# The last weight rows of a decode layer accumulated by column halves in two PSUM banks, with the output copy split over two engines

## The chip, the cores and the metric

One Trainium2 chip, one core. The time is the device time of the core in microseconds (us). "Span" is the part of the run that the profile covers (136.1 us of 138.0 for the kernel before). PE is TensorE (PEld its weight loads), DVE VectorE, ACT ScalarE, SP SyncE; L485 is line 485 of the kernel, and lines move by a few between versions.

## The reference, cut to what matters

One decode step of a transformer layer for four sequences: attention over the last 2048 cached positions, then a gated MLP. Only the end matters here:

```python
h  = x + attention(layernorm(x))          # h is h1 in the kernel, [4, 1024]
h_ = silu(hn @ w1) * (hn @ w3)            # hn = layernorm(h); w1, w3: 1024 x 3584
h2 = h + h_ @ w2                          # w2: 3584 x 1024, all bfloat16
```

## The kernel before

The kernel keeps a ring in SBUF and streams all weights and the cache through it in one fixed order on SyncE's DMA queue. w2 comes last, as 28 "rows" (one row is 128 partitions x 1024 columns), in four loads:

```python
("w2", load_rows, (56 * KIB, w2_v, D, 0, 17)),     # rows 0 to 16
("w2", load_rows, (90 * KIB, w2_v, D, 17, 7)),     # rows 17 to 23
("w2", load_rows, (104 * KIB, w2_v, D, 24, 3)),    # rows 24 to 26
("w2", load_rows, (110 * KIB, w2_v, D, 27, 1)),    # row 27
```

The 1024 output columns are folded into four groups of 256, one to each strip of 32 partitions, so that one row is four matmuls with 32 columns of weights each, which run side by side: within a row of the first load the four start within 34 ns of each other and the record of each lasts 0.37 to 0.42 us, while rows follow each other every 213 ns at a granted clock of 0.50. h1 enters the accumulation early, through a matmul with an fp32 identity. At the end ScalarE copies the PSUM bank and issues the store:

```python
# early, while VectorE computes the layernorm statistics
nc.tensor.matmul(y2_ps[:], lhsT=ident_f[:], rhs=h1[:], start=True, stop=False, ...)
# ... gate and up projections, hgT = transposed product ... (cut)
for i in range(IF):                       # 28 rows of w2
    for j in range(JG):                   # 4 strips
        nc.tensor.matmul(y2_ps[QD * j : QD * (j + 1), :], lhsT=hgT[:, i, :],
                         rhs=loaded["w2"][i][:, j * CG : (j + 1) * CG],
                         start=False, stop=(i == IF - 1), ...)
res = act.tile([P, CG], BF16)
nc.scalar.copy(out=res[:], in_=y2_ps[:])
nc.scalar.dma_start(out=out_flat..., in_=res[0:P:RS, :])
```

## Time and profile before

| Kernel before | value |
|---|---|
| time, median of 3 runs | 138.03 us (137.88 to 138.03) |
| read from HBM | 55.59 MB, 408 GB/s over the span |
| PE, DVE, ACT busy | 54%, 32%, 23% of the span |
| last load's landing to the issue of the store | 0.77 us |

Two rows of the page of the kernel before: the span in 40 slices, each digit a busy share (or granted clock) in tenths.

```profile
PEclk9999999999999999997555555579757777555577
DMA  5999999999999999999979999989899999989970
```

The DMA engines are nearly full from the second slice to almost the last (9 in most slices, 7 at the lowest); no compute engine is busy in all of them (PE, the busiest, 54%). The chain of work that ended last, of the kernel before, from 95 us on (start us, us, what):

```profile
75.97 22.91 DMA ring<-in_B_w_dram
98.88 0.04 issue
98.92 2.41 PE g_ps L455 x17
...
101.46 31.31 DMA ring<-in_B_w_dram
132.77 0.04 issue
132.81 0.32 PE y_ps L485 x4
133.13 0.02 issue
133.15 0.37 ACT res L495
```

So the kernel is a stream of bytes, and only what comes after the last byte can be shortened by work on the engines: four matmuls (0.32 us), one copy (0.37 us) and the store. The timeline of the kernel before at its end (start, duration, engine, line, operation, count, and in brackets the idle time before it and what ended it):

```profile
126.09 3.82 PE L485 MATMUL y_ps<-ring,hgT 128*32 128x256 bf16 x68 [7.08 <-DMA ring<-in_B_w_dram]
...
130.34 1.22 PE L485 MATMUL y_ps<-ring,hgT 128*32 128x256 bf16 x28 [0.43 <-DMA ring<-in_B_w_dram]
...
132.18 0.92 PE L485 MATMUL y_ps<-ring,hgT 128*32 128x256 bf16 x16 [0.63 <-DMA ring<-in_B_w_dram]
...
133.15 0.37 ACT L495 CAST res<-y_ps 128x256 bf16<-128x256 f32 x1 [26.41 <-PE y_ps L485]
133.55 0.60 ACTq L496 DMA_DIRECT2D out_dram<-res  x1
```

PE waits for the data of rows 0, 17 and 24. The third line holds rows 24 to 26 and row 27 together; the chain above shows that row 27 began at 132.81. PE thus has room of its own before row 24 (0.63 us).

### The profile page before, as it was taken

How to read it: one execution, taken by the hardware profiler on the slowest of the kernel's cores; microseconds unless marked ns; L12 is line 12 of the kernel's file. 1: busy time of each engine (PE TensorE's matmuls, PEld its weight loads, DVE VectorE, ACT ScalarE, POOL GpSimd, SP SyncE). 2: the span in 40 equal slices, each digit the busy share in tenths (PEclk: the TensorE clock that was granted, in tenths of full speed). 3: DMA queues.
4: the chain of work that ended last, by engine and by line, in shares of the span. 5: the costliest groups of instructions: out<-in, count | busy, mean ns of one | idle time of the engine just before them, and what ended most of it. 6: DMA issues, size and time to landing. Idle time of an engine off the chain costs nothing.

```text
span 136.1 us, 2343 instructions
## 1 busy us (share of the span) xinstructions
PE 73.8 (54%) x1050; PEld 45.0 (33%) x1050; DVE 43.4 (32%) x79; ACT 31.1 (23%) x36; POOL 1.7 (1%) x8
## 2 busy tenths in 40 slices
PE   0202980979898989810535906793096440900960
PEld 0200220267474747400024905571043210300840
DVE  6820000044243434471984001206100695080000
ACT  3000000016555555518385200000002300000001
POOL 5000000000000000000000000000000000000000
PEclk9999999999999999997555555579757777555577
DMA  5999999999999999999979999989899999989970
GB/s 156 463 464 404 404 438 405 424 428 438 433 428 419 429 443 428 429 522 477 462 327 443 481 409 404 477 371 477 354 430 426 438 455 442 430 389 419 421 288 5
DMA packets 2789, 55.75 MB, mean 410 GB/s; under 512 B 311, under 2 KB 471, under 8 KB 731
## 3 DMA queue, kind: packets, MB, share of 16 engines
q1 hardware_dynamic: 2731, 55.58, 95.6%
q8 instruction: 8, 0.13, 0.3%
q10 hardware_dynamic: 48, 0.02, 0.1%
q14 instruction: 2, 0.02, 0.0%
HBM read 55.59 MB, written 0.01 MB: 408 GB/s over the span
## 4 chain that ended last, share of the span: by engine, by line
DMA 54%; PE 24%; ACT 11%; DVE 5%; SPq 2%; issue 1%; ACTq 0%
DMA ring<-in_B_w_dram 40%; DMA ring<-in_A_wq_dram 15%; PE kt_ps L315 10%; ACT kT L321 5%; PE scores_ps L300 5%; ACT z L356 3%; PE q_ps L259 3%; SPq L119 2%; PE g_ps L455 2%; DVE rmax L332 2%; ACT Pm L337 2%; PE OT_ps L378 2%; DVE pT L346 1%; DVE z L352 1%; ACT L337 1%
## 5 line engine op out<-in xcount | busy, mean ns | idle before, releaser
L321 ACT COPY kT<-kt_ps 128x1024 bf16<-128x1024 bf16 x16 | 15.9, 1013 | 13.1 <-PE kt_ps L315 13.1
L315 PE MATMUL kt_ps<-ident,ring 128*128 128x128 bf16 x256 | 17.8, 230 | 0.0
L315 PEld LDWEIGHTS <-ring 128*128 128x128 bf16 x256 | 15.8, 104 | 4.9 <-issue 4.9
L319 DVE COPY kT<-kt_ps 128x1024 bf16<-128x1024 bf16 x16 | 11.1, 692 | 16.2 <-PE kt_ps L315 16.2
L259 PE MATMUL q_ps<-ring,xnT 128*4 128x512 bf16 x63 | 7.2, 626 | 10.5 <-DMA ring<-in_A_wq_dram 10.5
L378 PE MATMUL OT_ps<-z,ring 128*128 128x32 bf16 x256 | 7.5, 188 | 9.0 <-ACT z L356 5.0
L455 PEld LDWEIGHTS <-hnT 128*32 128x32 bf16 x128 | 5.3, 137 | 19.3 <-issue 16.6
L300 PE MATMUL scores_ps<-kT,qz 128*32 128x512 bf16 x64 | 9.9, 610 | 2.9 <-ACT kT L321 2.9
L455 PE MATMUL u_ps<-ring,hnT 128*32 128x448 bf16 x64 | 6.4, 576 | 8.2 <-DMA ring<-in_B_w_dram 8.2
L378 PEld LDWEIGHTS <-ring 128*128 128x128 bf16 x256 | 7.4, 105 | 9.8 <-issue 9.7
L485 PE MATMUL y_ps<-ring,hgT 128*32 128x256 bf16 x112 | 5.8, 375 | 8.3 <-DMA ring<-in_B_w_dram 8.1
L455 PE MATMUL g_ps<-ring,hnT 128*32 128x448 bf16 x64 | 5.5, 529 | 5.2 <-DMA ring<-in_B_w_dram 5.2
L485 PEld LDWEIGHTS <-hgT 128*32 128x32 bf16 x112 | 4.5, 130 | 10.2 <-issue 5.9
L259 PEld LDWEIGHTS <-xnT 128*4 128x4 bf16 x63 | 2.0, 115 | 14.8 <-issue 14.7
L277 DVE TENSOR_SCALAR q_sb<-q_ps 128x512 bf16<-128x512 f32 x1 | 0.7, 692 | 19.5 <-PE q_ps L259 19.5
L495 ACT CAST res<-y_ps 128x256 bf16<-128x256 f32 x1 | 0.4, 372 | 26.4 <-PE y_ps L485 26.4
L356 ACT ACTIVATE z<-pt_ps,mask 128x512 bf16<-128x512 f32 x8 | 5.3, 687 | 3.5 <-DVE z L352 3.5
L348 PE MATMUL pt_ps<-pT,perm 128*128 128x512 bf16 x4 | 2.4, 608 | 6.8 <-DVE pT L346 6.8
L278 ACT ACTIVATE q_sb<-q_ps 128x512 bf16<-128x512 f32 x1 | 0.6, 597 | 23.6 <-DVE q_sb L277 23.6
L405 PE MATMUL y_ps<-ring,o 128*32 128x256 bf16 x128 | 5.5, 352 | 0.8 <-DVE o L394 0.8
L352 DVE TENSOR_SCALAR z<-pt_ps,mask 128x512 bf16<-128x512 f32 x8 | 5.5, 738 | 1.2 <-ACT z L356 0.8
L469 DVE RECIPROCAL eg<-eg 128x896 f32<-128x896 f32 x1 | 5.8, 5754 | 0.0
(79 smaller groups left out, 50.2 us busy)
## 6 DMA issues: line engine op xcount, KB each, us to landing
ring<-in_A_k_cache_dram SPq DMA_DIRECT2D x4, 2048.0 KB, 25.4
ring<-in_A_v_cache_dram SPq DMA_DIRECT2D x4, 2048.0 KB, 39.0
ring<-in_B_w_dram SPq DMA_DIRECT2D x1, 7168.0 KB
ring<-in_B_w_dram SPq DMA_DIRECT2D x2, 3584.0 KB, 23.3
ring<-in_B_w_dram SPq DMA_DIRECT2D x1, 4352.0 KB
ring<-in_A_wq_dram SPq DMA_DIRECT2D x1, 4096.0 KB, 12.1
ring<-in_A_wq_dram SPq DMA_DIRECT2D x1, 3968.0 KB, 19.8
ring<-in_B_w_dram SPq DMA_DIRECT2D x1, 1792.0 KB
```

The source lines that it names most:

```text
L259: nc.tensor.matmul(q_ps[QD * g : QD * g + B, hf * 512 : hf * 512 + n], lhsT=xnT[:, kc, :], rhs=wq_t[:, c0 : c0 + n], start=(kc == 0), stop ...
L300: nc.tensor.matmul(scores_ps[QD * g : QD * (g + 1), n * 512 : (n + 1) * 512], lhsT=qz_v[:, z0 : z0 + QD], rhs=kT_v[:, g, :, :], start=(b = ...
L315: nc.tensor.transpose(out=kt_ps[:, jj, :], in_=k_v[:, n * NJ + t * TB + jj, :], identity=ident[:])
L319: nc.vector.tensor_copy(out=kT[:, t * TB : (t + 1) * TB, :], in_=kt_ps[:])
L321: nc.scalar.copy(out=kT[:, t * TB : (t + 1) * TB, :], in_=kt_ps[:])
L352: nc.vector.tensor_scalar(out=z[:, :, g, :], in0=pt_ps[:], scalar1=mask[:, g : g + 1], scalar2=None, op0=ALU.mult)
L356: nc.scalar.mul(out=z[:, :, g, :], in_=pt_ps[:], mul=mask[:, g : g + 1])
L378: nc.tensor.matmul(OT_ps[:, b, :], lhsT=loaded["v"][b][:, j, :], rhs=PTz[j // NJ][:, (j % NJ) * B + b, :, :], start=(j == 0), stop=(j == J ...
L405: nc.tensor.matmul(y_ps[QD * j : QD * (j + 1), :], lhsT=o4[:, i, :, :].rearrange("p b s -> p (b s)"), rhs=loaded["wo"][i][:, j * CG : (j + ...
L455: nc.tensor.matmul(out_ps[QD * j : QD * (j + 1), hf, :HF], lhsT=hnT[:, k, :], rhs=loaded[kind][k][:, c0 : c0 + HF], start=(k == 0), stop=( ...
L469: nc.vector.reciprocal(out=eg[:], in_=eg[:])
L485: nc.tensor.matmul(y2_ps[QD * j : QD * (j + 1), :], lhsT=hgT[:, i, :], rhs=loaded["w2"][i][:, j * CG : (j + 1) * CG], start=False, stop=(i ...
```

## The change

The intent: shorten the copy after the last matmul by giving half the columns to VectorE and half to ScalarE. The two halves lie in two PSUM banks, one for each engine; that the second bank is needed was the assumption. To keep the bulk of the rows in whole-width matmuls, rows 0 to 16 go into the freed bank `y`, VectorE adds h1 to them, and the sum joins the two halves through the fp32 identity after row 23.

```diff
-    y2_ps = psB.tile([P, CG], FP32, tag="y2")
+    HC = CG // 2
+    ya_ps = psB.tile([P, 512], FP32, tag="ya")
+    yb_ps = psB.tile([P, 512], FP32, tag="yb")
...
-    nc.tensor.matmul(y2_ps[:], lhsT=ident_f[:], rhs=h1[:], start=True, ...)
...
+    y2_ps = psB.tile([P, CG], FP32, tag="y")
+    h2 = wide.tile([P, CG], FP32, tag="w4k")
+    # down(i, n, c0, out_ps): the four strips of row i, n columns from c0 (cut)
+    for i in range(R1):                                   # R1, R2 = 17, 24
+        down(i, CG, 0, y2_ps, start=(i == 0), stop=(i == R1 - 1))
+    nc.vector.tensor_tensor(out=h2[:], in0=y2_ps[:], in1=h1[:], op=ALU.add)
+    for i in range(R1, IF):
+        for c, t in enumerate((ya_ps, yb_ps)):
+            down(i, HC, c * HC, t, start=(i == R1), stop=(i == IF - 1), ...)
+        if i == R2 - 1:
+            for c, t in enumerate((ya_ps, yb_ps)):
+                nc.tensor.matmul(t[:, :HC], lhsT=ident_f[:],
+                                 rhs=h2[:, c * HC : (c + 1) * HC], start=False, stop=False, ...)
-    nc.scalar.copy(out=res[:], in_=y2_ps[:])
+    nc.vector.tensor_copy(out=res[:, :HC], in_=ya_ps[:, :HC])
+    nc.scalar.copy(out=res[:, HC:], in_=yb_ps[:, :HC])
```

More of the change, by code (lines that the diff above doesn't have):

```diff
@@ L80 @@
     RING = 5 * 16384
+    R1, R2 = 17, 24
     RQ = 4
@@ L445 @@
     )
-    nc.tensor.matmul(y2_ps[:], lhsT=ident_f[:], rhs=h1[:], start=True, stop=False, skip_group_check=True)
     def gate_up(kind, out_ps):
@@ L480, with down @@
     )
-    for i in range(IF):
+    y2_ps = psB.tile([P, CG], FP32, tag="y")
+    h2 = wide.tile([P, CG], FP32, tag="w4k")
+    def down(i, n, c0, out_ps, **kw):
         for j in range(JG):
             nc.tensor.matmul(
-                y2_ps[QD * j : QD * (j + 1), :],
+                out_ps[QD * j : QD * (j + 1), :n],
                 lhsT=hgT[:, i, :],
-                rhs=loaded["w2"][i][:, j * CG : (j + 1) * CG],
-                start=False,
-                stop=(i == IF - 1),
-                skip_group_check=True,
-            )
+                rhs=loaded["w2"][i][:, j * CG + c0 : j * CG + c0 + n],
+                **kw,
+            )
+    for i in range(R1):
[3 more added lines that the diff above has]
+        for c, t in enumerate((ya_ps, yb_ps)):
+            down(i, HC, c * HC, t, start=(i == R1), stop=(i == IF - 1), skip_group_check=True)
+        if i == R2 - 1:
+            for c, t in enumerate((ya_ps, yb_ps)):
+                nc.tensor.matmul(
+                    t[:, :HC], lhsT=ident_f[:], rhs=h2[:, c * HC : (c + 1) * HC],
+                    start=False, stop=False, skip_group_check=True,
+                )
     res = act.tile([P, CG], BF16)
-    nc.scalar.copy(out=res[:], in_=y2_ps[:])
+    nc.vector.tensor_copy(out=res[:, :HC], in_=ya_ps[:, :HC])
+    nc.scalar.copy(out=res[:, HC:], in_=yb_ps[:, :HC])
     nc.scalar.dma_start(out=out_flat.rearrange("b (j c) -> j b c", j=JG), in_=res[0:P:RS, :])
```

## The prediction

> **What bounds the kernel now.** Bytes. The page gives 55.59 MB read at 408 GB/s over a 136.1 us span; its DMA row is at 9 in most slices. From 76 us on the chain of waits is two DMA pieces (22.9 and 31.3 us) with 2.4 us of gate matmuls between, while the queue still has a backlog. The weights of w2 come last. In the timeline PE waits for each piece: rows 0 to 16 start at 126.09, 17 to 23 at 130.34, 24 to 26 at 132.18, row 27 at 132.81. The exposed tail starts there: four 256-column matmuls (0.32 us), a ScalarE copy of 128x256 (0.37 us), issue of the store at 133.55, and 2.5 us of store and end, untouched.
>
> **What the change does.** The loads, their order and waits stay the same, so row 27 should land at about 132.8 again. Off the path it removes the fp32 identity matmul at 92.3 us (0.70 us on PE; nobody waits for it) and adds a 128x256 VectorE add after row 16 (the residual add of that shape took 425 ns), done long before it is needed.
>
> *Saved on the path.* The final copy becomes two 128x128 copies on two engines. A ScalarE copy of 128x128 from PSUM took 265 ns here, against 372 ns for 128x256; VectorE handled 128x128 from PSUM in 292 ns and may start about 50 ns earlier. Saving about 0.1 us. The last row is eight matmuls of half the columns: same streaming.
>
> *Added, perhaps on the path.* Rows 17 to 27 double their instructions (44 more weight loads and matmuls). The four column strips run together: rows follow each other every 107 to 110 ns at clock 1.00 and 213 ns at 0.50[...]. I expect half rows at 55 to 65 ns, as 128-wide weight loads with 32 columns go by every 27 ns in attention. But a weight load's record lasts 92 to 97 ns (150 at half clock); if that can't overlap two half rows deep, a row costs about 200 ns. Then two fp32 identity matmuls of 128 columns come between rows 23 and 24. One of 256 columns took 0.70 us, so two of 128 are estimated at 0.6 to 0.8 us[...].
>
> Before, PE ended rows 17 to 23 at 131.56 and idled 0.63 us. The identity pair about fills that gap: row 24 starts near 132.3 rather than 132.18, rows 24 to 26 issue in 0.35 us, still before row 27 lands. So nothing is added. In the bad case PE is late by 0.5 to 0.7 us at the end.
>
> **Prediction.** 138.0 us (about 0.1 saved, against a chance of one in four of losing 0.3 to 0.7), 137.6 to 138.7 in 8 of 10. Faster by over 2%: 0.01; within 2%: 0.98; slower: 0.01.
>
> **What would show it.** Right: PE idle before row 27 with DMA as releaser; the chain ends DMA, eight matmuls, ScalarE copy of about 0.27 us, store issued about 0.1 us earlier after the landing; half rows 55 to 65 ns apart at full clock. Wrong: no DMA wait before row 27, PE back to back from row 17 to the end.
>
> **What would make it wrong.** A low granted clock in the last 6 us (it rose from 0.50 to 1.00 only at 130.94; later, and the identity pair and half rows cost twice as much);[...] weight loads that bind; or DMA time differing by more than the 0.1 us seen between runs.

The pair's 0.6 to 0.8 us held extra cost, with no figure of its own; the figure that is shown is the 0.70 us of one identity matmul of 256 columns. The pair was set against the 0.63 us gap before row 24 and counted as nothing added, so the sum came to the 138.03 us of the kernel before, less about 0.1, with a chance of one in four of losing 0.3 to 0.7: put down as 138.0. The 50 ns by which VectorE may start earlier were an estimate without a stated source; 0.06 us were measured.

## More of the kernel before

In the waits of the kernel before, PE has a long one for which no releaser is named ("issue"; the columns are us in total, times, and the longest):

```profile
PE OT_ps L378 <- issue: 4.0, 1, 4.0
```

## The result, and the profile after

The changed kernel took 137.87 us (median of 6 runs, 137.77 to 137.94), the kernel before 138.03 us in the same rounds (6 runs, 137.86 to 138.07). The ratio is 0.9991, with a 95% interval of 0.9978 to 1.0003. Ratios here are the mean time of one kernel's fast runs over that of the other's of the same rounds, so not quite the ratio of the medians quoted beside them.

The chain of work that ended last, of the changed kernel, from 95 us on:

```profile
98.95 2.41 PE g_ps L456 x17
...
101.49 31.30 DMA ring<-in_B_w_dram
132.79 0.04 issue
132.83 0.24 PE ya_ps L489 x4
133.07 0.08 PE yb_ps L489 x4
133.16 0.02 issue
133.18 0.27 ACT res L511
```

Up to the last landing nothing moved: 132.79 us here, 132.77 before. The matmuls of row 27 take 0.32 us in sum, as before, and the copy 0.27 us in place of 0.37. The timeline of the changed kernel at its end:

```profile
130.37 0.30 PE L489 MATMUL ya_ps<-ring,hgT 128*32 128x128 bf16 x4 [0.34 <-DMA ring<-in_B_w_dram]
...
130.68 0.23 PE L489 MATMUL ya_ps<-ring,hgT 128*32 128x128 bf16 x4
130.74 0.23 PE L489 MATMUL yb_ps<-ring,hgT 128*32 128x128 bf16 x4
130.79 0.23 PE L489 MATMUL ya_ps<-ring,hgT 128*32 128x128 bf16 x4
...
131.35 0.49 PE L504 MATMUL ya_ps<-h,ident_f 128*128 128x128 f32 x2
...
131.67 0.39 PE L504 MATMUL yb_ps<-h,ident_f 128*128 128x128 f32 x2
...
132.21 0.24 PE L489 MATMUL ya_ps<-ring,hgT 128*32 128x128 bf16 x4 [0.15 <-DMA ring<-in_B_w_dram]
...
132.83 0.24 PE L489 MATMUL ya_ps<-ring,hgT 128*32 128x128 bf16 x4
...
132.89 0.24 PE L489 MATMUL yb_ps<-ring,hgT 128*32 128x128 bf16 x4
133.12 0.29 DVE L510 CAST res<-ya_ps 128x128 bf16<-128x128 f32 x1 [2.62 <-PE yb_ps L489]
133.18 0.27 ACT L511 CAST res<-yb_ps 128x128 bf16<-128x128 f32 x1 [26.60 <-PE yb_ps L489]
133.49 0.60 ACTq L512 DMA_DIRECT2D out_dram<-res  x1
```

A half row is the four matmuls of 128 columns of one row that go to one bank. Half rows follow each other 55 to 56 ns apart once the clock is up. The identity pair sits in what was idle time before row 24, and PE still waits 0.15 us for that row's data. VectorE starts its half 0.06 us ahead of ScalarE and both end within 0.04 us.

From the issue of the store to the end of the span takes 2.57 us in both traces (133.554 to 136.125 us before, 133.486 to 136.060 after), so the store issued 0.07 us earlier ended the span 0.07 us earlier.

The whole saving is small against the scatter of a run, so I use a measure from the trace that the scatter of the DMA hardly touches (0.678, 0.678 and 0.679 us in the three traces of the changed kernel), the **tail**: from the instant at which SyncE's record in the trace shows the last load as landed (0.02 to 0.03 us ahead of row 27's first matmul where PE is waiting) to the start of the store's issue. It is 0.767 us before and 0.678 us after: 0.089 us less.

### The profile page after: what moved, and what is told of

Same layout as the page of the kernel before. It is cut to its first block, busy times and chain, and to the rows that moved or that the text cites. A ratio compares the mean times of both kernels' runs of the same rounds, so it can differ in the third digit from the quotient of the medians.

```text
span 136.1 us, 2438 instructions
## 1 busy us (share of the span) xinstructions
PE 72.9 (54%) x1096; PEld 45.1 (33%) x1096; DVE 44.1 (32%) x81; ACT 31.0 (23%) x36; POOL 1.7 (1%) x8
## 4 chain that ended last, share of the span: by engine, by line
DMA 55%; PE 23%; ACT 11%; DVE 5%; SPq 2%; issue 1%; ACTq 0%
DMA ring<-in_B_w_dram 40%; DMA ring<-in_A_wq_dram 15%; PE kt_ps L316 10%; ACT kT L322 5%; PE scores_ps L301 5%; ACT z L357 3%; PE q_ps L260 3%; SPq L120 2%; PE g_ps L456 2%; DVE rmax L333 2%; ACT Pm L338 2%; PE OT_ps L379 2%; DVE pT L347 1%; DVE z L353 1%; ACT L338 1%
## 5 line engine op out<-in xcount | busy, mean ns | idle before, releaser
L489 PE MATMUL y_ps<-ring,hgT 128*32 128x256 bf16 x68 | 3.8, 418 | 7.2 <-DMA ring<-in_B_w_dram 7.2
```

Of the source, the lines that this page charges most:

```text
L489: nc.tensor.matmul(out_ps[QD * j : QD * (j + 1), :n], lhsT=hgT[:, i, :], rhs=loaded["w2"][i][:, j * CG + c0 : j * CG + c0 + n], **kw,)
```

## The experiments

All outputs were correct. Each tail is that of one traced execution. Times are medians of 5 or 6 runs, ratios are to the kernel before on the same chip and rounds.

| Run | what it is | tail, us | median, us | ratio (95%) |
|---|---|---|---|---|
| kernel before | | 0.767 | 138.03 | |
| changed kernel, e0_after | again | 0.678 | 137.95 | 0.9995 (0.9981 to 1.0009) |
| changed kernel, e11_after_again | and again | 0.679 | 137.79 | 0.9986 (0.9974 to 0.9999) |
| e1_one_copy | one ScalarE copy | 0.770 | 137.96 | 0.9997 (0.9984 to 1.0010) |
| e2_copies_only | halves for all rows, early h1 | 0.889 | 138.06 | 1.0011 (0.9991 to 1.0030) |
| e3_join_late | identity pair after row 26 | 1.148 | 138.39 | 1.0028 (1.0012 to 1.0044) |
| e5_three_pairs | two more pairs | 1.026 | 138.55 | 1.0034 (1.0011 to 1.0057) |
| e4_store_sync | store from SyncE | see below | 138.21 | 1.0012 (0.9999 to 1.0025) |
| e8_pad_mid | 88 PE instructions after row 16 | 0.890 | 139.04 | 1.0065 (1.0042 to 1.0089) |
| e9_pad_early | the same ahead of row 0 | 0.679 | 138.32 | 1.0034 (0.9997 to 1.0071) |
| e10_copies_padded | e2 with them ahead of row 0 | 0.679 | 137.87 | 1.0008 (0.9976 to 1.0039) |

**The changed kernel again.** No edit.

> The changed kernel again, as the yardstick of these rounds. Tail = from the first matmul of row 27 to the issue of the store: 0.65 to 0.66 us (before: 0.74). Time 0.1 to 0.15 us under before (ratio near 0.9991).

> The changed kernel once more, beside the padded copies-only kernel: tail 0.68 us from the landing of row 27 to the store, ratio to before 0.999 to 1.000.

The tail came out as 0.678 and 0.679 us. The three ratios to the kernel before (0.9991, 0.9995, 0.9986) all lie under 1; only the last interval excludes it. A saving of 0.09 us would be a ratio of 0.9994.

**Is it the copy?**

```diff
-    ya_ps = psB.tile([P, 512], FP32, tag="ya")
-    yb_ps = psB.tile([P, 512], FP32, tag="yb")
+    yab_ps = psB.tile([P, 2, 512], FP32, tag="yab")
+    ya_ps, yb_ps = yab_ps[:, 0, :], yab_ps[:, 1, :]
...
-    nc.vector.tensor_copy(out=res[:, :HC], in_=ya_ps[:, :HC])
-    nc.scalar.copy(out=res[:, HC:], in_=yb_ps[:, :HC])
+    nc.scalar.copy(out=res[:].rearrange("p (c n) -> p c n", c=2), in_=yab_ps[:, :, :HC])
```

> The changed kernel with its final copy on ScalarE alone, both banks in one instruction of 128x256. Theory (the saving is the shorter final copy): the copy takes about 0.37 us again, tail 0.74 to 0.76 us, time that of before, ratio 1.000. Rival (the saving comes from taking the identity matmul out of the 92 us stage and the new accumulation): tail may lengthen, but the time stays at ratio 0.999 because row 27 lands or starts earlier.

The timeline of ScalarE in this run:

```profile
133.39 0.37 ACT L510 CAST res<-yab_ps 128x256 bf16<-128x256 f32 x1 [26.81 <-PE yab_ps L489]
133.79 0.60 ACTq L511 DMA_DIRECT2D out_dram<-res  x1
```

The copy takes 0.37 us again and the tail is back at 0.770 us, with everything else of the change in place. The split copy is the saving. The total could not tell this: 137.96 us beside 137.95 for the changed kernel in the same rounds.

**Is the late join of rows 0 to 16 needed?** The edit starts from the kernel before: two banks, two early identity matmuls, all 28 rows in halves, split copies.

```diff
-    nc.tensor.matmul(y2_ps[:], lhsT=ident_f[:], rhs=h1[:], start=True, stop=False, ...)
+    for c, t in enumerate((ya_ps, yb_ps)):
+        nc.tensor.matmul(t[:, :HC], lhsT=ident_f[:], rhs=h1[:, c * HC : (c + 1) * HC], start=True, ...)
...
     for i in range(IF):
-        for j in range(JG):
-            nc.tensor.matmul(y2_ps[strip j, :], ..., rhs=loaded["w2"][i][:, CG columns])
+        for c, t in enumerate((ya_ps, yb_ps)):
+            for j in range(JG):
+                nc.tensor.matmul(t[strip j, :HC], ..., rhs=loaded["w2"][i][:, HC columns from c * HC])
```

> The kernel before with all 28 rows accumulated by column halves in two banks, h1 joined early by two identity matmuls as before, and the split final copies; no VectorE add, no late identity pair. Theory: it keeps the whole saving, tail 0.65 to 0.66 us, ratio near 0.9991; the late join of rows 0 to 16 buys nothing. Rival: without the late join the ratio goes back to 1.000. If half rows cost more at half clock than at full clock, rows 0 to 16 take clearly over 3.82 us, but PE would still wait for rows 24 to 26.

My theory missed here: the tail is 0.889 us, longer than before. The two copies are as short as in the changed kernel, but the timeline of PE shows why they start late:

```profile
131.31 0.23 PE L493 MATMUL ya_ps<-ring,hgT 128*32 128x128 bf16 x2
132.45 0.23 PE L493 MATMUL ya_ps<-ring,hgT 128*32 128x128 bf16 x2 [0.91 <-issue]
132.45 0.28 PE L493 MATMUL yb_ps<-ring,hgT 128*32 128x128 bf16 x4
```

PE stops for 0.91 us between the second and the third strip of one half row, in the middle of rows 17 to 23, whose data had landed more than 1 us before. No semaphore wait stands there. When it resumes, three and a half half rows of rows 17 to 23 and all of rows 24 to 27 are still to do, and row 27's data (landed at 132.755 us) waits for PE. Rows 0 to 16 themselves ran as fast as in whole rows: half rows 107 ns apart at half clock, which is 213 ns a row as before.

**Where the stall comes from.** The waits of the kernel before show such a stop too ("issue", 4.0 us, in the attention stage). I numbered PE's recorded instructions (weight loads, matmuls and its few semaphore instructions) in the traces. All twelve traces, the kernel before and the changed kernel among them, stop ahead of number 1216 (2.8 to 4.2 us of idle time in the six whose waits I listed: 4.0 before, 4.2 in the changed kernel, 4.0 in e2, 2.8 in e8, 3.2 in e9, 3.9 in e10); e1 and e2 also ahead of 1472 (1.3 us in e2); e2 ahead of 2240 (0.91 us). These are 256 and 3 x 256 apart. The DMA part of the page counts packets of an "instruction" queue (packets, MB, share), first in the kernel before, then in the copies-only kernel:

```profile
q8 instruction: 8, 0.13, 0.3%
```

```profile
q8 instruction: 9, 0.15, 0.4%
```

Each packet is 16384 bytes. My reading is that one packet brings the next 256 instructions of PE, and that PE stops when they come late. No record says what a packet holds, so this rests on the spacing, the count of packets and their times. The times fit: the packet that precedes the restart at 1216 in the kernel before began at 80.08 us and PE resumed at 82.35; for 2240 in the copies-only kernel 129.97 and 132.45.

The times of the packets tell more. In all twelve traces there are as many packets as boundaries passed (numbers 192, 448 and so on by 256 to 1984, which is 8, or 9 where PE passes 2240). All but one of them begin 0.7 to 6.0 us after PE passes a boundary, and the shortest time from there to PE's first instruction after the following boundary is 2.2 us. So the packet that follows 1984 seems to bring what begins at 2240, and PE stops when it gets through a block faster than the next one comes: in the copies-only kernel it passed 1984 at 127.31 us and had come to 2240 some 4 us later, 1 us before it could go on. DMA engines busy with weights are a likely reason for packets that come so late, but this was not tested. The changed kernel ends at number 2195, so it never gets to 2240. Two runs test the reading that PE lacked instructions. Both add 44 one-column matmuls, 88 instructions, whose result nobody reads:

```diff
+    def pad():
+        for k in range(11):
+            for j in range(JG):
+                nc.tensor.matmul(sums_ps[QD * j : QD * (j + 1), 0:1], lhsT=hgT[:, k, :],
+                                 rhs=<one column of row 16, or of hgT>, start=True, stop=True, ...)
     for i in range(R1): down(i, CG, 0, y2_ps, ...)
     nc.vector.tensor_tensor(out=h2[:], in0=y2_ps[:], in1=h1[:], op=ALU.add)
+    pad()          # e8; in e9 it stands ahead of the loop over rows 0 to 16
```

> The changed kernel with 44 tiny matmuls (88 PE instructions, one column each, into a bank nobody reads any more) between row 16 and row 17, where PE waits for data. Theory for the idle time in the copies-only kernel: PE ran out of instructions. Its stalls without a named releaser stand before its recorded instructions number 1216, 1472 and 2240, which are 256 apart[...]. The changed kernel has only 2196 recorded PE instructions, so it never gets to 2240; here 2240 falls into row 25, and the fetch starts near 130.6 us as in the changed kernel. Expected: PE idle without a releaser from about 132.4 to about 133.0 us, before instruction 2240, store about 0.4 us later after the landing of row 27, ratio to before about 1.002. Rival (the stall came from half rows for rows 0 to 16, or from the clock): no idle time there, at most 0.2 us added, ratio 0.999 to 1.000.

> The same 44 tiny matmuls ahead of row 0, at about 122 us, where PE waits for w2 anyhow. The number of PE instructions is that of the run with the padding in the middle. Theory: instruction 1984, one packet ahead of 2240, is now passed about 2.5 us earlier (row 2 in place of row 13), so the packet is fetched 1 to 2.5 us earlier and is there before row 25: no idle time before 2240, ratio near 0.999. Rival (the number of instructions alone costs the time): same loss as with the padding in the middle.

With the padding after row 16, the chain of work that ended last contains this:

```profile
132.74 0.05 PE ya_ps L489 x2
132.79 0.23 issue
133.02 0.23 PE ya_ps L489 x2
```

PE started its next matmul at 133.02, 0.47 us after the last one (132.55), ahead of instruction 2240 exactly, 2.2 us after the packet that began at 130.83. The tail is 0.890 us. It is 0.21 us longer than in the changed kernel, where I expected about 0.4, since row 27 landed 0.19 us later in this run than in the changed kernel (132.997 against 132.808 us) and hid about that much of it. With the same padding ahead of row 0, PE passed 1984 at 126.55 us and the packet began at 129.74. The timeline of PE around 2240 (132.34 us, in the first of these half rows):

```profile
132.33 0.24 PE L489 MATMUL ya_ps<-ring,hgT 128*32 128x128 bf16 x4
132.39 0.24 PE L489 MATMUL yb_ps<-ring,hgT 128*32 128x128 bf16 x4
132.44 0.24 PE L489 MATMUL ya_ps<-ring,hgT 128*32 128x128 bf16 x4
```

PE did not stop, 2.6 us after the packet began, and the tail is 0.679 us. So it is not the number of instructions but, by this reading, where the boundary falls and when its packet can come.

The totals of these two runs missed what I expected: 1.0065 in place of 1.002, and 1.0034 (with an interval that includes 1) in place of 0.999. I cannot explain that fully. In 9 of their 12 runs the time exceeds the span by 2.0 to 3.3 us, in all other runs here by 1.7 to 1.9 us. The profiled run with the padding in the middle (139.50 us, span 136.5) shows a ninth instruction packet at 138.76 us, after the end of the span; the profiled run with the padding ahead (137.83 us, span 136.1) has its ninth at 133.19. That suggests that the end of the program waits for a fetch of instructions beyond it. It was not tested and stays open. Because of it, the ratios of these two runs are not used for the tail.

**The same padding in the copies-only kernel.**

> The copies-only kernel with the same 44 tiny matmuls ahead of row 0. If PE ran out of instructions at number 2240 in the copies-only kernel, 88 more instructions ahead of row 0 make it better: 2240 now falls at the end of row 16 and 1984 is passed before row 0 (at 122 to 126 us), so the packet comes in time. Expected: no idle time without a releaser in rows 17 to 27, PE waits for data before row 24 and row 27 again, tail from row 27's landing to the store 0.68 us as in the changed kernel (copies-only: 0.89), which would show that the split copies alone give the saving and the late join is there for the instruction count. Rival (halves for all 28 rows are slow in themselves): the tail stays at 0.85 us or more.

The edit is the padding of e9 in e2: 88 more instructions ahead of row 0. The timeline of PE:

```profile
130.26 0.30 PE L500 MATMUL ya_ps<-ring,hgT 128*32 128x128 bf16 x4 [0.44 <-DMA ring<-in_B_w_dram]
...
131.31 0.23 PE L500 MATMUL yb_ps<-ring,hgT 128*32 128x128 bf16 x4
132.11 0.24 PE L500 MATMUL ya_ps<-ring,hgT 128*32 128x128 bf16 x4 [0.56 <-DMA ring<-in_B_w_dram]
```

The stop is gone, PE waits for data before row 24 (0.56 us), and the tail is 0.679 us, that of the changed kernel. The kernel with more instructions has the shorter tail. So halves for all rows are as good as the late join in the tail, and the stall of e2 was, by the same reading, its instruction supply. Five of its six runs took 137.71 to 137.93 us; one took 139.37 with a span of 137.6, and I have no trace of that one.

**How much room does the identity pair have?** First its place:

```diff
-    R1, R2 = 17, 24
+    R1, R2 = 17, 27
```

> The changed kernel with the identity pair moved from behind row 23 to behind row 26 (one constant). Theory (the pair costs PE about 0.75 us from the last half row to the next weight load, and is free only because PE waits for data there): PE has 0.27 us of wait before row 27, so row 27 starts about 0.5 us after it has landed; tail counted from the landing 1.15 to 1.2 us instead of 0.68, time about 0.5 us over the changed kernel, ratio to before about 1.0027. Rival (a pair is cheap wherever it stands): ratio stays at 0.999.

The timeline of PE in this run:

```profile
132.71 0.24 PE L489 MATMUL yb_ps<-ring,hgT 128*32 128x128 bf16 x4
132.88 0.49 PE L504 MATMUL ya_ps<-h,ident_f 128*128 128x128 f32 x2
133.21 0.39 PE L504 MATMUL yb_ps<-h,ident_f 128*128 128x128 f32 x2
133.53 0.24 PE L489 MATMUL ya_ps<-ring,hgT 128*32 128x128 bf16 x4
```

From one half row to the next take 0.82 us with the pair between, against 0.055 without. Row 27 starts 0.49 us after its landing (133.04), the tail is 1.148 us, and the time is 0.28% up, as expected. The pair is not cheap; it is free where the change puts it. Then its size, with two more pairs of zeros (`zf` a zero tile) in the same place:

```diff
+            for c, t in enumerate((ya_ps, yb_ps) * 2):
+                nc.tensor.matmul(t[:, :HC], lhsT=ident_f[:], rhs=zf[:, :HC], start=False, stop=False, ...)
```

> The changed kernel with two more identity pairs behind row 23 that add zeros (the result stays right). Each extra pair is estimated at 0.43 us of PE (four passes of 107 ns). The trace after shows 0.15 us of wait before row 24 and 0.27 us before row 27, 0.42 us in all. Theory: 0.86 us more work minus 0.42 us of slack leaves row 27 late by about 0.45 us, no wait before row 24 or row 27, ratio to before about 1.0025. Rival (PE has far more room there): ratio 0.999.

The timeline of PE at the last pass of zeros and the first half row of row 24:

```profile
132.65 0.39 PE L511 MATMUL yb_ps<-zf,ident_f 128*128 128x128 f32 x2
132.96 0.24 PE L491 MATMUL ya_ps<-ring,hgT 128*32 128x128 bf16 x4
```

PE has no wait left before rows 24 and 27, and the tail is 1.026 us, 0.35 us over the changed kernel (0.45 expected). The total rose by 0.34% (0.25% expected). The eight extra passes (the trace records two for each fp32 matmul) ran 0.112 us apart, where 107 ns had been estimated without a stated source, 0.89 us in all, so the change leaves a reserve of about 0.54 us before the last row (0.89 less 0.35; 0.42 was read from the trace). The late join fits the part of it before row 27: 0.76 us of pair less 0.27 us of wait is 0.49. Of those 0.76 us about 0.45 are the pair's four passes, at the 0.112 us of the passes of zeros. The other 0.3 us is an estimate from these two numbers of what going from half rows to the pair and back costs; no run shows what it consists of.

**A cheaper store?** Issuing the store from SyncE, which is idle by then:

```diff
-    nc.scalar.dma_start(out=out_flat..., in_=res[0:P:RS, :])
+    nc.sync.dma_start(out=out_flat..., in_=res[0:P:RS, :])
```

> The changed kernel with the output store issued by SyncE in place of ScalarE. In the trace of before, issuing a DMA took ScalarE 0.60 us and SyncE 0.33 us late in the kernel. If the transfer starts when the issue is complete, the end comes 0.2 to 0.27 us earlier: ratio about 0.997 to 0.998. If the transfer's start doesn't depend on the issue's length, no change against the changed kernel: ratio 0.999.

The end of this run's timeline:

```profile
132.93 0.24 PE L489 MATMUL ya_ps<-ring,hgT 128*32 128x128 bf16 x4
...
133.58 0.65 SPq L512 DMA_DIRECT2D out_dram<-res  x1
```

Neither expectation held. The issue took 0.65 us here, not the 0.33 us of SyncE's load issues, and started as early as in the changed kernel (0.65 us after row 27's first matmul). But from the issue to the end of the span it took 2.84 us (133.58 to 136.43), against 2.57 us in the changed kernel (133.47 to 136.04), and the median was 0.26 us higher (138.21 against 137.95). The longer part lies in the closing steps after the data has landed: 0.99 us from SyncE's record of the landing to the start of its last event, against 0.76 us. Why they are longer was not pursued.

No run beat the changed kernel's tail.

## Why the prediction was right

The total alone could not show it: a saving of 0.09 us is below the scatter, and the predicted range (137.6 to 138.7 us) also holds the medians of the kernel before, e3 and e5. The tail and the traces are the evidence.

- *Bytes bound the kernel, and the landing of row 27 does not move.* Right: 132.77 and 132.79 us in the chains.
- *0.1 us saved on the path, through the copy.* Right in size and place: 0.089 us of tail. ScalarE's half took 266 ns (265 were read from a copy of the same shape), VectorE's 291 (292). Taking the split away gives it all back (0.770 us).
- *The last row in halves costs the same.* Right: 0.32 us in both chains (0.24 and 0.08 in the changed kernel).
- *Half rows at 55 to 65 ns; weight loads do not bind.* Right: 55 to 56 ns at full clock and 107 ns at half clock, although each weight load's record lasts 92 to 150 ns.
- *The identity pair at 0.6 to 0.8 us, hidden before row 24.* Right: 0.76 us more between two half rows where it is exposed (0.82 less 0.055). The predicted start of row 24 was a little late (132.3, measured 132.21 with 0.15 us of idle time left), in part because the full clock was granted at 130.6 us and not at 130.9 as in the trace before.
- *A low clock in the last 6 us as a danger.* Not seen in the three traces of the changed kernel, where the full clock was granted from 130.6, 129.9 and 128.7 us on; its other 14 executions have no trace, and all 17 took 137.71 to 138.16 us. In the trace of e3 the clock rose only at 132.1 us; half rows 107 ns apart still ended before row 24's data, but no pair stood in that gap there. Pair and low clock together remain untested: that the pair would cost twice as much was carried over from rows (213 ns apart at a clock of 0.50, 107 to 110 at 1.00).
- *What the prediction did not see:* it counted the 44 added weight loads and matmuls only as work on PE. They also lengthen PE's instruction stream. The changed kernel ends 44 recorded instructions short of a boundary at which two other versions stop for 0.5 to 1.1 us from one matmul's start to the next. That the change keeps rows 0 to 16 whole is what keeps it short of it. The prediction was right there by luck: it had no reason for it.

## What to carry to other kernels

In a kernel bound by its loads, look at what follows the last landing; a two-engine copy there is worth just its own shortening (0.09 us of 138), and extra work is free only if it fits into a wait that you can point to. Read idle time without a releaser on PE as a possible lack of instructions: number the instructions, look for a spacing of 256 (here 1216, 1472 and 2240, with idle time of 0.2 to 4.2 us), and look at the times of the instruction packets (ahead of 1216 in the kernel before and in the changed one, and ahead of 2240 in e2 and e8, PE resumed 2.2 to 2.5 us after the start of the last one). Where the saving is below the scatter of the total, measure an interval in the trace that starts after the scattered part.
